# A fused attention and two-layer feed-forward kernel: one w_in unit, w_out's units and block 0's y change their places

## The chip, the cores and the metric

One core of one Trainium2 chip. The metric is the device time of one execution in microseconds (us). Engines: TensorE (PE, with its weight loads PEld), VectorE (DVE), ScalarE (ACT), GpSimd (POOL), and SyncE (SP), whose queue issues the DMAs here.

## What is computed

Four batches of 8-head attention (half of the heads with a local mask, half with a strided one), a first feed-forward part without a nonlinearity between its products, and a second one with a sigmoid gelu:

```python
# attention: q, k, v of 4 x 8 x 576 x 64, masks per head
x = softmax(scale * q @ k.T, masked) @ v       # 2304 tokens x 512
a = x @ w1                                     # 512 x 1024
b = x @ w2
y = (a * b @ w3) @ w_out                       # 1024 x 1024, 1024 x 512
h = y @ w_in                                   # 512 x 2048
out = (h / (1 + exp(-1.702 * h))) @ w_out2     # 2048 x 512
```

All in float32.

## The kernel before

Products run on TensorE at reduced operand width, so that every float32 factor is split into a high part (ScalarE, L246, `split_hi`) and a low part (VectorE, L252, `split_lo`), and each product is three matmuls (high x low, low x high, high x high). The weights arrive as raw 64-bit words and are turned into float32 on ScalarE and VectorE. The large last product, with w_in and w_out of the second part, is done by a fast matrix scheme with seven products of quarters, for which sums of the weights' quarters are made first.

The weights of that last part are converted in eight units each, in stages in which TensorE is doing something else:

- w_in units (`u_placed`, L1098): two conversions on ScalarE (L1111, L1112), three steps on VectorE (L1113 to L1115), the sums (L1106, L1093, L1108), a write-back to DRAM (L1117), and the load of the unit two further on (L1088). Their places are in `UNITS_Y` (batch 1's y) and `UNITS_2` (batch 2).
- w_out units (`wo_steps`, L1120): two conversions (ScalarE, L1144, L1145), three steps on VectorE (L1146 to L1148), three sums (L1133, L1093), two high splits (`high`, ScalarE), two low splits (`low`, VectorE), two stores (L1128). Unit 0 is made at the end of batch 2's stage from `EARLY_AT` on, units 1 to 6 in batch 3's stage, unit 7 in the last one.

The stages around the change, by the time in the profile: batch 1's y (201 to 260), batch 2's products with the last attention pairs (260 to 334), the end of batch 2's y and batch 3 (334 to 429), the last products (429 on). Within a stage every engine's order is written by hand: each piece of work has a place in units of one TensorE step of 12 matmuls, the pieces are sorted by place, and each engine (TensorE, VectorE, ScalarE, SyncE) runs its own in that order and waits only for what it needs:

```python
for _, _, f in sorted((at, n, f) for n, (at, f) in enumerate(steps)):
    f()
```

A product pair (`pieces`, L1224) of batch 2 or 3 for chunk m of 8 and half hb has its places from `at = 24 * hb + 2 * m`: first product (`one(0)`, at), its copy by ScalarE out of the accumulator (L1234, at + 0.99), second product (at + 1), multiply by VectorE (L1237, at + 1.99), high split (at + 2.4), low split (at + 2.75). The eight pairs of a half feed its y products (L1173; in batch 3 `fourth`, L1354): in the first half at steps 16 to 24, in batch 2's second half they are moved to the start of batch 3's list (`over`, places less 48, from -8), behind everything of batch 2's. The accumulators (`mm`) rotate over four.

An attention pair (`placed`, L673) at place u has the products of the pair before and its own scores on TensorE (`trip`), the mask and maximum on VectorE (L546), exponentials on ScalarE (L556), the normalisation (L565 to L567), 32x32 transposes on VectorE for a local head (L583) or on TensorE for a strided one (L589). Pair 10 has two local ones; pair 11 is only the last product.

Block 0's y for the last part is read back in two halves kk and split in `y_steps` (L1312), placed at `at + gaps`. `early_y` (L1283) opens the space for it and issues the loads of w_out unit 1 and of y; `early_load` issues that of unit 0; `wo_load` those of units 2 to 6, each into a space that an earlier piece has to leave first.

Of the kernel before, what the change touches and what calls it, by code (L numbers as in the profile page):

```python
# [51 lines left out]
BODY = 0x7FFFFFF8  # L52
REBIAS = 2.0 ** -112
LOW = 2.0 ** -29
PAIRS_Y = ((4, 2.6), (5, 12.8), (6, 25.6))
UNITS_Y = ((0, 8.3), (1, 17.0), (2, 21.2), (3, 30.3))
PAIRS_2 = ((7, 2.4), (8, 10.6), (9, 19.8), (10, 28.4), (11, 37.0))
UNITS_2 = ((4, 6.4), (5, 15.6), (6, 24.2), (7, 31.8))
PAIR_AT = (0.05, 0.12, 0.2, 0.32, 0.42, 0.55, 0.72)
EARLY = 8  # L60
EARLY_AT = 35.6
AHEAD = 6
PACED = 50
MOVED = {
# [148 lines left out]
def body(ctx: ExitStack, tc, qk, vv, mask, ql, vl, qs, vs, qmask, w1, w2, w3t, wo, win, wout, out):  # L213
# [27 lines left out]
    def r(ap):  # L241
        return ap.bitcast(F32)
# [75 lines left out]
    def room(what, n, w, tag, bufs):  # L318
        if what + str(n) in lent:
            return lent[what + str(n)]  # L320
        return aq.tile([P, w], F32, tag=tag, name=tag, bufs=bufs)
# [769 lines left out]
    def both_minus(out, a, x):  # L1091

        nc.vector.tensor_tensor(  # L1093
            out.rearrange("p (n c) -> p n c", n=2), a.unsqueeze(1).to_broadcast([P, 2, 256]),
            x[:, :7 * 256].rearrange("p (n c) -> p n c", c=256)[:, 0:5:4], op=ALU.subtract,
        )
# [20 lines left out]
            (u + 3, sums), (u + 4.2, lambda: nc.sync.dma_start(widram[i], x[:, 256:])),  # L1117
        ]

    def wo_steps(u, raw, room, high_room=None, late=0):  # L1120
        view = lambda t: raw().bitcast(t).rearrange("p (n t) -> p n t", t=2)
        hi = lambda: (high_room or raw)().bitcast(F32R)[:, :7 * 256]
        xi = lambda: room()[:, :CW2].bitcast(I32)
        part = lambda n: room()[:, n * 256:(n + 1) * 256]
        B12, B11, B21, B22, S1, S3, S2 = range(7)

        def store(s, t):
            nc.sync.dma_start(  # L1128
                tdram[:, u // 2, :, u % 2, s].rearrange("j p n -> p j n"), t.rearrange("p (j n) -> p j n", j=7)
            )  # L1130

        def sum_(o, a, b, op):
            nc.vector.tensor_tensor(part(o), part(a), part(b), op=op)  # L1133

        def low(n):
            c = slice(n * 896, (n + 1) * 896)
            split_lo(room()[:, c].bitcast(F32R), room()[:, c], hi()[:, c])

        def high(n):
            c = slice(n * 896, (n + 1) * 896)  # L1140
            split_hi(hi()[:, c], room()[:, c])

        return [
            (-0.6, lambda: nc.scalar.activation(view(I32)[:, :, 0], view(U32)[:, :, 0], AF.Copy, scale=LOW)),  # L1144
            (0.1, lambda: nc.scalar.activation(room()[:, :CW2], view(F32)[:, :, 1], AF.Copy, scale=REBIAS)),  # L1145
            (0.8, lambda: nc.vector.tensor_scalar(xi(), xi(), 3, BODY, op0=ALU.logical_shift_left, op1=ALU.bitwise_and)),  # L1146
            (1.25, lambda: nc.vector.scalar_tensor_tensor(xi(), view(I32)[:, :, 1], SIGN, xi(), op0=ALU.bitwise_and, op1=ALU.bitwise_or)),
            (2.05, lambda: nc.vector.tensor_tensor(xi(), xi(), view(I32)[:, :, 0], op=ALU.add)),  # L1148
            (2.65 + late / 2, lambda: sum_(S1, B12, B22, ALU.add)),
            (2.75 + late / 2, lambda: both_minus(room()[:, 5 * 256:7 * 256], part(B11), room())),  # L1150
            (3.1 + late / 2, lambda: sum_(B12, B21, S2, ALU.add)),
            (3.45 + late, lambda: high(0)),
            (3.9 + late, lambda: high(1)),
            (4.05 + late, lambda: low(0)),
            (4.35 + late, lambda: store(0, r(hi()))),
            (4.8 + late, lambda: low(1)),
            (5.4 + late, lambda: store(1, room()[:, :7 * 256])),
        ]

    cvs = ExitStack()  # L1160
# [137 lines left out]
            early[1] = cv[0].tile([P, 2 * CW2], F32, tag="x", name="x", bufs=2)  # L1298
        return early[1]

    steps2 += [(27.0, early_load), (38.6, early_y)]
    steps2 += [(EARLY_AT + g, f) for g, f in wo_steps(0, lambda: early[0], early_room, None, 1.6)]
    written(steps2)
    cvs.close()
    xbs_stack.close()
# [74 lines left out]
    )  # L1380
    sums = early["sums"]
    steps3.append((-6.9, lambda: ys.update({0: y_load(0, 0, rooms[1])})))
    for kk, at in ((1, -0.9), (0, 2.2)):
        gaps = (0.05, 1.0, 1.4, 0.1, 0.75, 0.8, 1.85, 2.0, 2.85)
        steps3 += [(at + g, f) for g, f in zip(gaps, y_steps(kk, ys))]

    def wo_load(u):
        todo3[u] = rooms[(0, 1, 2, 0, 1, 0)[u - 2]]()
        nc.sync.dma_start(todo3[u], wout[u])

    UNIT = 8.0
    for u in range(1, NU):
        at = -5.8 if u == 1 else 6 + UNIT * (u - 2)
        if 1 < u < NU - 1:
            steps3.append((((2.6, 5.5, 5.7)[u - 2] if u < 5 else at - 14), lambda u=u: wo_load(u)))
        if u < NU - 1:
            steps3 += [(at + g, f) for g, f in wo_steps(u, lambda u=u: todo3[u], lambda u=u: sums[:, u % 2])]
    for n, (lo, hi, a, b, c) in enumerate(((4, 6, 32.1, 40.2, 41.6), (5, 7, 40.05, 46.9, 47.7))):
        lo, hi = slot[lo][:, :7 * 256], slot[hi][:, :7 * 256]
        steps3 += [  # L1400
# [57 lines left out]
    class Split:  # L1458
# [4 lines left out]
        def hi(self):  # L1463
            self.t = self.room or p2.tile([P, 2, HT], F32R, tag="sp", name="sp", bufs=7)
            split_hi(self.t[:, 0], self.src())
# [304 lines left out]
```

## Time and profile before

| what | us |
|---|---|
| median of 3 runs | 791.58 |
| the runs | 789.95, 791.58, 793.72 |
| the profiled execution | 791.2 |
| its span, first to last instruction | 789.4 |
| TensorE busy | 770.6 (98%) |
| VectorE busy | 580.8 (74%) |
| ScalarE busy | 480.2 (61%) |
| mean granted TensorE clock | 0.996 of 2.4 GHz |

The span is that of one execution, with some 1.8 us around it. A row of an instruction list has its start and duration; what stands in brackets is how long the engine had been idle and what ended that. A row of the table of waits says who waited for whom. In the busy tables a stretch is given with the busy us of each engine, the granted share of TensorE's clock (1.00 is 2.4 GHz, 0.50 is 1.2 GHz) and the DMA engines' share.

### The profile page before, as it was taken

The page shows a single profiled execution, that of the slowest core. Times are in us where ns is not written, and L with a number is a line of the kernel's source. Part 1 is how long each engine was busy: PE and PEld are TensorE (multiplying, and loading weights), DVE is VectorE, ACT ScalarE, POOL GpSimd, SP SyncE. Part 2 cuts the span into 40 slices and gives each one's busy share as a digit, 9 for nine tenths or more (in the row PEclk, how much of TensorE's full clock was granted, in tenths as well). Part 3 has the DMA queues.
Part 4 walks back from the last instruction along what each step waited for, and adds up shares of the span by engine and source line. Part 5 has one row for each costly group of instructions (what it writes and reads, how often), then busy time and mean ns, then how long its engine had stood idle before and what let it go on. Part 6 is the DMA issues. An engine that isn't in the chain of part 4 may idle for free.

```text
span 789.4 us, 16754 instructions
## 1 busy us (share of the span) xinstructions
PE 770.6 (98%) x6545; PEld 747.6 (95%) x6545; DVE 580.8 (74%) x1248; ACT 480.2 (61%) x1041; POOL 5.8 (1%) x14
## 2 busy tenths in 40 slices
PE   5899999999999999989999999999999999999998
PEld 4899999987999999988999999999999999999998
DVE  4899678788778686977776788794677794577743
ACT  5877646477565554554465767673666674666552
POOL 2000000000000000000000000000000000000000
PEclk9999999999999999999999999999999999999999
DMA  8887455632788546296998837789254489343382
GB/s 281 293 307 237 163 172 176 206 125 83 255 270 285 176 144 218 83 296 203 243 274 235 329 134 249 285 280 383 105 203 150 155 282 374 113 160 112 113 280 89
DMA packets 72078, 168.14 MB, mean 213 GB/s; under 512 B 6336, under 2 KB 45248, under 8 KB 69440
## 3 DMA queue, kind: packets, MB, share of 16 engines
q1 hardware_dynamic: 71856, 167.04, 63.2%
q8 instruction: 51, 0.84, 0.4%
q14 instruction: 27, 0.22, 0.1%
q10 hardware_dynamic: 144, 0.04, 0.0%
HBM read 130.88 MB, written 36.18 MB: 212 GB/s over the span
## 4 chain that ended last, share of the span: by engine, by line
PE 84%; DMA 5%; DVE 4%; ACT 4%; issue 1%; SPq 1%; ACTq 0%; DVEq 0%
PE acc L1508 23%; PE ps L1497 22%; PE ps L716 20%; PE ps L1173 8%; PE acc L1354 3%; PE acc L1019 3%; PE sc L533 1%; DMA sums<-ydram 1%; PE pv L602 1%; DMA tdram<-raw 1%; DMA raw<-in_wout 1%; ACT w L246 1%; DVE w L252 1%; DVE xw L809 1%; ACT xw L801 1%
## 5 line engine op out<-in xcount | busy, mean ns | idle before, releaser
L1508 PE MATMUL acc<-w,sp 128*128 128x256 f32 x1440 | 179.5, 282 | 0.0
L1508 PEld LDWEIGHTS acc<-w,sp 128*128 128x128 f32 x1440 | 177.8, 191 | 0.0
L1497 PE MATMUL ps<-yq,hl 128*128 128x384 f32 x924 | 168.1, 335 | 0.0
L1497 PEld LDWEIGHTS ps<-yq,hl 128*128 128x128 f32 x924 | 158.7, 188 | 0.9 <-DVE part L1453 0.6
L252 DVE TENSOR_TENSOR sp<-part,sp 128x384 fp32r<-128x384 f32 x136 | 71.5, 554 | 59.1 <-ACT sp L246 59.1
L716 PE MATMUL ps<-xbh,w 128*128 128x288 f32 x512 | 102.6, 295 | 0.0
L716 PE MATMUL ps<-xah,w 128*128 128x288 f32 x512 | 102.2, 294 | 0.0
L716 PEld LDWEIGHTS ps<-xbh,w 128*128 128x128 f32 x512 | 81.9, 188 | 1.3 <-issue 0.7
L1173 PE MATMUL ps<-ab,w 128*128 128x288 f32 x576 | 80.7, 300 | 2.2 <-DVE ab L252 2.1
L716 PEld LDWEIGHTS ps<-xah,w 128*128 128x128 f32 x512 | 82.0, 188 | 0.0
L1173 PEld LDWEIGHTS ps<-ab,w 128*128 128x128 f32 x576 | 78.2, 191 | 3.3 <-DVE ab L252 2.4
L716 PE MATMUL ps<-xal,w 128*128 128x288 f32 x256 | 76.5, 299 | 1.3 <-ACT abf L1234 0.7
L716 PE MATMUL ps<-xbl,w 128*128 128x288 f32 x256 | 76.9, 300 | 0.6 <-issue 0.6
L1450 ACT ACTIVATE part<-part 128x384 f32<-128x384 f32 x72 | 37.9, 526 | 61.4 <-DVE part L1453 61.3
L246 ACT ACTIVATE sp<-part 128x384 fp32r<-128x384 f32 x136 | 64.1, 517 | 11.3 <-PE acc L1508 10.3
L246 ACT ACTIVATE ab<-abf 128x288 fp32r<-128x288 f32 x64 | 27.3, 439 | 39.5 <-DVE abf L1237 37.1
L716 PEld LDWEIGHTS ps<-xal,w 128*128 128x128 f32 x256 | 48.0, 188 | 2.6 <-ACT abf L1234 1.1
L716 PEld LDWEIGHTS ps<-xbl,w 128*128 128x128 f32 x256 | 48.0, 188 | 0.9
L1019 PE MATMUL acc<-w,w 128*128 128x512 f32 x192 | 45.6, 396 | 0.2
L1019 PEld LDWEIGHTS acc<-w,w 128*128 128x128 f32 x192 | 35.8, 188 | 9.2 <-ACT raw L1025 1.0
L252 DVE TENSOR_TENSOR hl<-fetched,hl 128x1024 fp32r<-128x1024 f32 (+1 forms) x40 | 43.3, 1083 | 0.0
L246 ACT ACTIVATE w<-xw 128x512 fp32r<-128x512 f32 (+1 forms) x30 | 23.3, 775 | 29.2 <-DVE xw L809 28.3
(193 smaller groups left out, 1117.3 us busy)
## 6 DMA issues: line engine op xcount, KB each, us to landing
w<-tdram SPq DMA_DIRECT2D x84, 512.0 KB, 4.6
fetched<-widram SPq DMA_DIRECT2D x20, 896.0 KB, 6.2
raw<-in_win SPq DMA_DIRECT2D x8, 1024.0 KB, 5.5
widram<-x SPq DMA_DIRECT2D x8, 896.0 KB, 5.5
raw<-in_wout SPq DMA_DIRECT2D x7, 1024.0 KB, 5.2
tdram<-raw SPq DMA_DIRECT2D x6, 896.0 KB, 5.5
tdram<-sums SPq DMA_DIRECT2D x6, 896.0 KB
raw<-in_w3t SPq DMA_DIRECT2D x10, 512.0 KB, 4.5
```

What stands on the lines that cost most here:

```text
L246: nc.scalar.activation(hi, src, AF.Copy)
L252: e.tensor_tensor(lo, src, r(hi), op=ALU.subtract)
L533: nc.tensor.matmul(sc[:nq, g, i * P:i * P + nk], qs[rows, i], ks[rows, i], start=True, stop=True,)
L602: nc.tensor.matmul(pv[rows, h // 2, :nq], L["v"][:nk, h * D:(h + 1) * D], ps[:nk, h * nq:(h + 1) * nq], start=True, stop=True,)
L716: nc.tensor.matmul(ps, ws[a][m // 2][:, at:at + P], xh[c][:, k, cols], start=(k == 0 and (a, c) == ORDER[0]), stop=(k == KC - 1 and (a, c) ...
L801: "a": lambda xf, rf, ri, ru, x, hi, lo: nc.scalar.activation(xf, rf[:, :, 1], AF.Copy, scale=REBIAS),
L1019: nc.tensor.matmul(acc[f], hl[:, a, f * P:(f + 1) * P], wor[c][g], start=(g == 0 and (a, c) == ORDER[0]), stop=(g == MC - 1 and (a, c) == ...
L1173: nc.tensor.matmul(yacc[n], wfs[a][k][:, n * P:(n + 1) * P], hold[s % 2, k][:, c], start=(k == 0 and (a, c) == ORDER[0]), stop=(k == MC - ...
L1354: nc.tensor.matmul(st[0], wfs[a][k][:, n * P:(n + 1) * P], hold[hb, k][:, c], start=(k == 0 and (a, c) == ORDER[0]), stop=(k == MC - 1 and ...
L1450: nc.scalar.activation(out(), src(), func)
L1497: nc.tensor.matmul(ps, w[a][:, f * 256 + kk * P:f * 256 + (kk + 1) * P], yq[:, b, kk, c], start=(first and kk == 0 and (a, c) == ORDER[0]) ...
L1508: nc.tensor.matmul(to, g.t[:, a, t * P:(t + 1) * P], t3[:, i % 2, c], start=(opens and i == 0 and n == 0 and t % 2 == 0), stop=(i == NU - ...
```

## The change

Batch 1's y gets a fifth w_in unit (unit 4, from batch 2's list), its units and pairs are placed anew; batch 2 keeps units 5 to 7, and its pairs 9 to 11 come 0.8 to 1.4 steps sooner. `early_load` goes from 27.0 to 24.5, `early_y` from 38.6 to 37.4. w_out unit 0 begins at 34.9 instead of 35.6, and its sums, splits and stores are no longer set off by `late` (0.8 and 1.6 steps). In batch 3's list block 0's y halves go from -0.9 and 2.2 to -0.7 and 3.2, with smaller gaps; w_out's units 2 to 6 go from 6 + 8 (u - 2) to 8 + 7.75 (u - 2), the loads of units 3 and 4 go one step later, and from unit 2 on the second high split, the stores and the second low split stand half a step further behind.

```diff
--- before.py
+++ after.py
@@ -52,13 +52,13 @@
 BODY = 0x7FFFFFF8
 REBIAS = 2.0 ** -112
 LOW = 2.0 ** -29
-PAIRS_Y = ((4, 2.6), (5, 12.8), (6, 25.6))
-UNITS_Y = ((0, 8.3), (1, 17.0), (2, 21.2), (3, 30.3))
-PAIRS_2 = ((7, 2.4), (8, 10.6), (9, 19.8), (10, 28.4), (11, 37.0))
-UNITS_2 = ((4, 6.4), (5, 15.6), (6, 24.2), (7, 31.8))
+PAIRS_Y = ((4, 2.6), (5, 12.6), (6, 27.2))
+UNITS_Y = ((0, 8.0), (1, 16.6), (2, 20.2), (3, 24.0), (4, 31.4))
+PAIRS_2 = ((7, 2.4), (8, 10.6), (9, 19.0), (10, 27.2), (11, 35.6))
+UNITS_2 = ((5, 6.4), (6, 15.4), (7, 23.0))
 PAIR_AT = (0.05, 0.12, 0.2, 0.32, 0.42, 0.55, 0.72)
 EARLY = 8
-EARLY_AT = 35.6
+EARLY_AT = 34.9
 AHEAD = 6
 PACED = 50
 MOVED = {
@@ -1117,7 +1117,7 @@
             (u + 3, sums), (u + 4.2, lambda: nc.sync.dma_start(widram[i], x[:, 256:])),
         ]
 
-    def wo_steps(u, raw, room, high_room=None, late=0):
+    def wo_steps(u, raw, room, high_room=None, apart=0):
         view = lambda t: raw().bitcast(t).rearrange("p (n t) -> p n t", t=2)
         hi = lambda: (high_room or raw)().bitcast(F32R)[:, :7 * 256]
         xi = lambda: room()[:, :CW2].bitcast(I32)
@@ -1146,15 +1146,15 @@
             (0.8, lambda: nc.vector.tensor_scalar(xi(), xi(), 3, BODY, op0=ALU.logical_shift_left, op1=ALU.bitwise_and)),
             (1.25, lambda: nc.vector.scalar_tensor_tensor(xi(), view(I32)[:, :, 1], SIGN, xi(), op0=ALU.bitwise_and, op1=ALU.bitwise_or)),
             (2.05, lambda: nc.vector.tensor_tensor(xi(), xi(), view(I32)[:, :, 0], op=ALU.add)),
-            (2.65 + late / 2, lambda: sum_(S1, B12, B22, ALU.add)),
-            (2.75 + late / 2, lambda: both_minus(room()[:, 5 * 256:7 * 256], part(B11), room())),
-            (3.1 + late / 2, lambda: sum_(B12, B21, S2, ALU.add)),
-            (3.45 + late, lambda: high(0)),
-            (3.9 + late, lambda: high(1)),
-            (4.05 + late, lambda: low(0)),
-            (4.35 + late, lambda: store(0, r(hi()))),
-            (4.8 + late, lambda: low(1)),
-            (5.4 + late, lambda: store(1, room()[:, :7 * 256])),
+            (2.65, lambda: sum_(S1, B12, B22, ALU.add)),
+            (2.75, lambda: both_minus(room()[:, 5 * 256:7 * 256], part(B11), room())),
+            (3.1, lambda: sum_(B12, B21, S2, ALU.add)),
+            (3.45, lambda: high(0)),
+            (3.9 + apart, lambda: high(1)),
+            (4.05, lambda: low(0)),
+            (4.35 + apart, lambda: store(0, r(hi()))),
+            (4.8 + apart, lambda: low(1)),
+            (5.4 + apart, lambda: store(1, room()[:, :7 * 256])),
         ]
 
     cvs = ExitStack()
@@ -1298,8 +1298,8 @@
             early[1] = cv[0].tile([P, 2 * CW2], F32, tag="x", name="x", bufs=2)
         return early[1]
 
-    steps2 += [(27.0, early_load), (38.6, early_y)]
-    steps2 += [(EARLY_AT + g, f) for g, f in wo_steps(0, lambda: early[0], early_room, None, 1.6)]
+    steps2 += [(24.5, early_load), (37.4, early_y)]
+    steps2 += [(EARLY_AT + g, f) for g, f in wo_steps(0, lambda: early[0], early_room)]
     written(steps2)
     cvs.close()
     xbs_stack.close()
@@ -1380,21 +1380,21 @@
     )
     sums = early["sums"]
     steps3.append((-6.9, lambda: ys.update({0: y_load(0, 0, rooms[1])})))
-    for kk, at in ((1, -0.9), (0, 2.2)):
-        gaps = (0.05, 1.0, 1.4, 0.1, 0.75, 0.8, 1.85, 2.0, 2.85)
+    for kk, at in ((1, -0.7), (0, 3.2)):
+        gaps = (0.05, 0.8, 1.2, 0.1, 0.75, 0.8, 1.85, 1.9, 2.6)
         steps3 += [(at + g, f) for g, f in zip(gaps, y_steps(kk, ys))]
 
     def wo_load(u):
         todo3[u] = rooms[(0, 1, 2, 0, 1, 0)[u - 2]]()
         nc.sync.dma_start(todo3[u], wout[u])
 
-    UNIT = 8.0
+    UNIT = 7.75
     for u in range(1, NU):
-        at = -5.8 if u == 1 else 6 + UNIT * (u - 2)
+        at = -5.8 if u == 1 else 8 + UNIT * (u - 2)
         if 1 < u < NU - 1:
-            steps3.append((((2.6, 5.5, 5.7)[u - 2] if u < 5 else at - 14), lambda u=u: wo_load(u)))
+            steps3.append((((2.6, 6.5, 6.7)[u - 2] if u < 5 else at - 14), lambda u=u: wo_load(u)))
         if u < NU - 1:
-            steps3 += [(at + g, f) for g, f in wo_steps(u, lambda u=u: todo3[u], lambda u=u: sums[:, u % 2])]
+            steps3 += [(at + g, f) for g, f in wo_steps(u, lambda u=u: todo3[u], lambda u=u: sums[:, u % 2], None, 0.5 if u > 1 else 0)]
     for n, (lo, hi, a, b, c) in enumerate(((4, 6, 32.1, 40.2, 41.6), (5, 7, 40.05, 46.9, 47.7))):
         lo, hi = slot[lo][:, :7 * 256], slot[hi][:, :7 * 256]
         steps3 += [
```

## Rows read from the trace of the kernel before

**Rows 1.** Who waited for whom, TensorE: us in total, times, longest us.

```profile
PE ps L1173 <- DVE ab L252: 2.1, 1, 2.1
```

**Rows 2.** Busy table by stage: busy us (instructions) per engine, clock, DMA.

```profile
201.00:260.00 59.00, 58.96 (x495) 57.23 (x493) 46.05 (x142) 37.49 (x109) 0.00 (x0) 1.00 0.82 273
260.00:334.00 74.00, 74.00 (x638) 72.02 (x637) 59.16 (x185) 39.75 (x122) 0.00 (x0) 1.00 0.45 153
351.00:429.00 78.00, 76.75 (x574) 75.86 (x573) 58.07 (x86) 43.01 (x69) 0.00 (x0) 1.00 0.84 243
```

**Rows 3.** The same table in 2 us windows, behind the gap at 337.

```profile
340.00:342.00 2.00, 2.00 (x10) 2.00 (x9) 1.52 (x2) 2.00 (x4) 0.00 (x0) 0.50 0.45 146
342.00:344.00 2.00, 2.00 (x13) 2.00 (x12) 1.31 (x2) 0.63 (x1) 0.00 (x0) 0.69 1.11 271
```

**Rows 4.** TensorE's instructions in order: start, us, line, tile, [idle <-releaser].

```profile
329.97 0.88 PE L602 MATMUL pv<-band,v 128*64 128x96 f32 x16
334.04 2.92 PE L1173 MATMUL ps<-ab,w 128*128 128x288 f32 x21
339.09 6.18 PE L1173 MATMUL ps<-ab,w 128*128 128x288 f32 x33 [2.12 <-DVE ab L252]
...
366.99 0.40 PE L716 MATMUL ps<-xal,w 128*128 128x288 f32 x1 [0.36 <-ACT abf L1234]
...
369.41 0.40 PE L716 MATMUL ps<-xal,w 128*128 128x288 f32 x1 [0.58 <-DVE abf L1237]
...
374.95 0.40 PE L716 MATMUL ps<-xal,w 128*128 128x288 f32 x1 [0.30 <-ACT abf L1234]
```

**Rows 5.** VectorE's instructions, end of batch 2's stage.

```profile
315.67 0.29 DVE L546 CUSTOM_DVE_ANT_0 sm<-sc,msk 96x128 f32<-96x128 f32 x1 [2.96 <-PE sc L533]
...
323.13 0.45 DVE L1237 TENSOR_TENSOR abf<-ps,abf 128x288 f32<-128x288 f32 x1
323.50 1.87 DVE L583 STREAM_TRANSPOSE band<-sm 32x128 f32<-32x128 f32 x6
...
325.78 0.69 DVE L1113 TENSOR_SCALAR x<-x 128x1024 int32<-128x1024 int32 x1
...
331.03 0.45 DVE L1237 TENSOR_TENSOR abf<-ps,abf 128x288 f32<-128x288 f32 x1
331.40 0.68 DVE L1146 TENSOR_SCALAR x<-x 128x1024 int32<-128x1024 int32 x1
...
337.62 0.45 DVE L1237 TENSOR_TENSOR abf<-ps,abf 128x288 f32<-128x288 f32 x1
338.58 0.46 DVE L252 TENSOR_TENSOR ab<-abf,ab 128x288 fp32r<-128x288 f32 x1 [0.51 <-ACT ab L246]
339.42 2.10 DVE L252 TENSOR_TENSOR x<-x,raw 128x896 fp32r<-128x896 f32 x2 [0.38 <-ACT raw L246]
```

**Rows 6.** ScalarE's instructions, the same stretch and batch 3's first half.

```profile
328.12 0.45 ACT L246 ACTIVATE ab<-abf 128x288 fp32r<-128x288 f32 x1 [2.74 <-DVE abf L1237]
328.47 0.39 ACT L1234 ACTIVATE abf<-ps 128x288 f32<-128x288 f32 x1
328.76 1.16 ACT L1144 ACTIVATE raw<-raw 128x1024 int32<-128x1024 uint32 x1
329.81 1.17 ACT L1145 ACTIVATE x<-raw 128x1024 f32<-128x1024 f32 x1
...
338.45 1.78 ACT L246 ACTIVATE raw<-x 128x896 fp32r<-128x896 f32 x2
...
364.15 1.14 ACT L1144 ACTIVATE raw<-raw 128x1024 int32<-128x1024 uint32 x1 [2.33 <-DMA raw<-in_wout]
...
366.52 0.41 ACT L1234 ACTIVATE abf<-ps 128x288 f32<-128x288 f32 x1
```

**Rows 7.** The busy table in 2 us windows, in the opening.

```profile
20.00:22.00 2.00, 0.67 (x15) 0.54 (x14) 1.90 (x6) 0.91 (x2) 0.00 (x0) 1.00 0.95 326
22.00:24.00 2.00, 1.66 (x18) 1.54 (x18) 1.84 (x5) 1.92 (x6) 0.00 (x0) 0.60 0.84 284
```

## The prediction

> **What bounds the kernel now.** I read the waits of TensorE first, then the busy table by stage, then the instruction lists around each wait. TensorE waits for another engine for long only once after the opening: 2.1 us, for VectorE's `ab` [rows 1]. The table by stage shows it busy for 58.96 of 59 us in the stage of batch 1's y and for all 74 us of batch 2's products; in batch 3's stage it misses 1.25 of 78 us [rows 2]. So VectorE is worth something only where TensorE meets an empty input: at the seam of batches 2 and 3, and in batch 3's first half.
>
> The seam: batch 2's last y products start at 334.04, and TensorE stands from 336.97 to 339.09 [rows 4]. It wants the low split of the last product pair (m = 7), which VectorE ends at 339.04 [rows 5]. The product itself was there at 334.04; its multiply ran at 337.62, because w_out unit 0 stood ahead of it in VectorE's order. Then the clock falls from 2.4 to 1.2 GHz: the granted share is 0.50 from 340 to 342 and 0.69 from 342 to 344 [rows 3]. At half rate 2 x 0.50 + 2 x 0.31 = 1.62 us of work is lost there. The seam costs 2.12 + 1.62 = 3.74 us.
>
> Batch 3: three gaps of 0.36, 0.58 and 0.30 us [rows 4], together 1.24. ScalarE stood 2.33 us at w_out unit 2's first conversion, which waited for its load until 364.15, and the copy that frees TensorE's accumulator came behind it at 366.52 [rows 6]. All that the change can win is 3.74 + 1.24 = 4.98 us, 0.63% of the profiled execution's 791.2 us.
>
> **The change part by part.**
>
> *A w_in unit moves to batch 1's y.* In VectorE's list unit 7 begins at 325.78 and the next multiply at 331.03 [rows 5]; with two 0.37 us visitors taken out it costs 5.25 - 0.74 = 4.5 us. VectorE goes from 46.05 to some 50.6 busy of 59 us in the y stage and from 59.16 to 54.7 of 74 in batch 2's [rows 2]. The splits of y's input are placed four to five product steps ahead of their products; a step is 1.60 us (pair 11's product from 329.97, 0.88, and two steps fill the time to 334.04 [rows 4]); TensorE is full there now. The moved unit's load, its write-back and the two refills it triggers go with it on SP's queue, and the last y input loads (step 20) are ahead of the new unit (24.0). I cost it at 0; if a unit did push a split past its four steps (6.4 us), the bound is the whole unit, 4.5 us.
>
> *Unit 0 of w_out begins sooner.* Pair 10's attention goes from step 28.4 to 27.2, one product step: 315.67 - 1.60 = 314.07. From there to the multiply of m = 3 took 323.13 - 315.67 = 7.46 us; now its second transposes (1.87) stand ahead of that multiply, as does the multiply of m = 1 (0.37): 314.07 + 9.70 = 323.77 [rows 5]. From there ScalarE sets the pace: split of m = 3 at 324.25 (0.48 later, the multiply's 0.45 and a hand-over), copy at 324.60 (0.35, from 328.12 to 328.47), unit 0's first conversion at 324.89 (0.29), split of m = 4 at 325.94 (1.05), copy 326.29, second conversion 326.58, ready at 327.75 (1.17) [rows 6]. So VectorE begins unit 0 at 327.78 instead of 331.40 [rows 5]: 3.62 us sooner.
>
> *But its low splits now stand ahead of the last multiply.* With `late` gone they are placed at 38.95 and 39.70; before, at 41.25 and 42.0, behind it (39.99). From unit 0's first VectorE instruction to the end of the last low split took 339.04 - 331.40 = 7.64 us. Three things are added: the multiply of m = 5 (0.37, it stood just ahead at 331.03), the two splits (2.10, the row at 339.42) [rows 5], and a wait. ScalarE runs unit 0's first high split (38.35) ahead of the split of m = 6 (38.40), so VectorE, which wants m = 6 next, stands from the end of unit 0's sums: hand-over 0.10, high split 0.89 (half of 1.78 [rows 6]), split of m = 6 and hand-over 0.48, together 1.4. Queued behind that wait are unit 0's low splits and then the last multiply, for which TensorE waits. 327.78 + 7.64 + 0.37 + 2.10 + 1.4 = 339.3.
>
> So the head start of 3.62 is spent on 3.87 of work and waiting, and the last low split ends at 339.3 against 339.04. The unknown is how much of the 1.4 runs beside other waits. Bounds: none hidden, 339.3; all hidden, 337.9. A floor from TensorE agrees: the second conversion stands behind the copy of m = 5, whose product ends where step 35 begins, 334.04 less five steps and pair 11's 0.88, 325.16, which gives 325.16 + 0.3 + 0.3 + 1.17 = 326.9 and an end at 338.4 with the 1.4, 337.0 without. I take 339.3, +0.3 us, because nothing in the order lets ScalarE pass. The clock then falls as before: a gap as long at the same place.
>
> *The load of unit 1 and of y* are issued some steps sooner; unit 1's first conversion stands behind the split of m = 7 on ScalarE either way, and now without the 1.78 us of high splits between [rows 6]. Its stores and so the load of unit 2 come about a microsecond sooner. 0 by itself.
>
> *Block 0's y 1.0 step and unit 2 two steps further behind.* Unit 2's first conversion is placed at 7.4 instead of 5.4, behind the copy (6.99) that came at 366.52. That copy then follows the multiply of m = 2, and stands near 364.0, 2.6 us ahead of when TensorE wants the accumulator (366.99 - 0.36 = 366.63). The next multiply (7.99) is ahead of unit 2 on VectorE too. All three gaps go: -1.24. What is late next: unit 2 (from step 8) against the copy of m = 4, wanted three steps later; units 3 to 6 come at most 1.75 steps later with 7.75 between, the last ends near step 45 of 48, and its factors are held back until the next stage's sixth quad. If the unit blocks there again: 0 of the 1.24. `apart` lets the copy of the next m go between two high splits: 0.
>
> Sum on the profiled execution: 791.2 + 0.3 - 1.24 = 790.3. The median of the runs shown, 791.58, lies 0.4 above that execution, so 790.6 for the median.
>
> **The rivals.** *The gap shrinks and the clock stays.* If the 1.4 us wait hides and ScalarE has the conversions at its floor, the end is 337.0 to 338.4, a gap of 0 to 1.4. The opening has a gap of 1.33 us in the window 20 to 22, followed by a grant of 0.60 [rows 7], so it would have to be short. At a gap of 0.7: -1.42 - 1.62 - 1.24 = -4.3, 787.3 for the median; at none 786.6. For it: VectorE is 4.5 us emptier in this stage. Against: the order on ScalarE and the two splits in front.
>
> *The gap stays, the clock does not fall.* Then -0.94 - 1.62 = -2.6, 789.0. The trace shows one fall behind each of two long gaps [rows 3, 7], so I give it little. The Trainium skill, "TensorE: Matmul & The Clock Gate", Part 1, says that the gate's timing runs free of the kernel, so that one kernel can differ from run to run; by that rule the 1.62 us could fall away with the same gap. No run of before here shows a gap of 2 us without a fall.
>
> *Slower: the splits in front without the head start.* If ScalarE's conversion of unit 0 is held as it was (second conversion at 329.81 [rows 6]), unit 0 begins at 331.4 and the added 3.87 lie wholly on TensorE's gap: 2.12 becomes 6.0 us. With the 1.24 won: +2.6, and a second stretch at half rate as long as the first +1.6: 791.2 + 4.2, 795.8 for the median. It decides at unit 0's first VectorE instruction: break-even is 0.94 behind the forecast's place, 328.7; later than that is slower than before. The chain of ScalarE steps above speaks against; that the chain starts with a multiply VectorE reaches late speaks for.
>
> *The change does not do what it says in batch 3:* the gaps return at other units: 791.9.
>
> **How the numbers follow.** Forecast 0.57 (790.6, own range 789.3 to 791.8 with the runs' scatter); shrunk gap 0.17 (787.3); clock spared 0.11 (789.0); splits in front 0.09 (795.8); no gain in batch 3 0.06 (791.9). A measurement of this kernel tells about 0.5%, 4.0 us, from no change. Faster by more than that holds most of the second case, 0.14; slower most of the fourth, 0.08; the rest is 0.78. The range reaches from the middle of the shrunk gap, 786.8, to part of the slower case, 794.0.
>
> **What would show it.** In the changed profile: unit 0's first VectorE instruction near 327.8, its two 896-wide low splits ahead of the last multiply, TensorE's gap at 337 between 1.5 and 2.6 us with half clock behind it; ScalarE's copy of m = 3 ahead of unit 2's conversion and no gap between 366 and 376; VectorE some 50 of 59 us busy in the y stage with no gap of TensorE. The forecast is wrong if the gap at 337 is under 1 us or over 3.5, or if the y stage shows TensorE waiting.

## The result and the profile after

The changed kernel took 797.1 us in the median (795.78 to 798.37) against 791.7 for the kernel before beside it: a ratio of 1.0069, 95% interval 1.0057 to 1.0081. It is slower, where 790.6 with a range from 786.8 to 794.0 had been forecast. Its profiled execution has a span of 795.3 us, 5.9 more than before.

First the table of waits of TensorE after the opening (who waited for whom: us in total, times, longest):

```profile
PE ps L1497 <- ACT z L1562: 4.8, 1, 4.8
...
PE ps L1173 <- DVE ab L252: 2.2, 1, 2.2
...
PE pt L589 <- DVE sm L567: 0.8, 1, 0.8
...
PE ps L716 <- ACT abf L1234: 0.3, 1, 0.3
```

The second line is the seam's wait of [rows 1], still there. The first and the third are new: a stop of 4.8 us in the last stage, which no step of the prediction looks at, and one of 0.8 in the stage of batch 1's y. The same four in TensorE's list (start, us, line, tile, idle before and releaser), against [rows 4]:

```profile
261.89 0.62 PE L589 MATMUL pt<-ident,sm 126*126 126x126 f32 x4 [0.83 <-DVE sm L567]
...
341.50 3.70 PE L1173 MATMUL ps<-ab,w 128*128 128x288 f32 x26 [2.20 <-DVE ab L252]
...
412.30 0.40 PE L716 MATMUL ps<-xal,w 128*128 128x288 f32 x1 [0.33 <-ACT abf L1234]
...
428.30 5.82 PE L1497 MATMUL ps<-yq,w 128*128 128x384 f32 x30
438.94 8.15 PE L1497 MATMUL ps<-yq,w 128*128 128x384 f32 x36 [4.82 <-ACT z L1562]
```

The busy table of after by stage, as in [rows 2], and in 2 us windows, first behind the seam's gap, as in [rows 3], then around the new stop (busy us of PE, PEld, DVE, ACT, POOL, granted share of the clock, DMA share, GB/s):

```profile
201.00:260.00 59.00, 58.97 (x490) 56.98 (x489) 47.97 (x142) 38.23 (x111) 0.00 (x0) 1.00 0.86 292
260.00:334.00 74.00, 73.17 (x631) 71.00 (x630) 59.69 (x188) 40.09 (x123) 0.00 (x0) 1.00 0.45 159
```

```profile
340.00:342.00 2.00, 0.50 (x4) 0.50 (x4) 0.93 (x3) 1.46 (x2) 0.00 (x0) 1.00 1.09 263
342.00:344.00 2.00, 2.00 (x18) 2.00 (x17) 0.34 (x1) 1.43 (x2) 0.00 (x0) 1.00 1.16 299
...
436.00:438.00 2.00, 0.00 (x0) 0.00 (x0) 0.00 (x0) 0.00 (x0) 0.00 (x0) 0.50 0.98 308
438.00:440.00 2.00, 1.06 (x3) 1.07 (x4) 0.67 (x2) 0.90 (x2) 0.00 (x0) 0.50 1.04 368
440.00:442.00 2.00, 2.00 (x8) 2.00 (x8) 0.91 (x2) 0.67 (x2) 0.00 (x0) 0.50 0.96 386
442.00:444.00 2.00, 2.00 (x12) 2.00 (x11) 1.52 (x2) 1.39 (x3) 0.00 (x0) 0.87 1.03 428
```

Behind the seam's gap the clock stayed at 2.4 GHz this time; from within the stop in the last stage it was at 1.2 GHz until about 442.5.

Where the 5.9 us of the two profiled executions come from, by the starts of TensorE's stages:

| up to | before | after | later by | of it |
|---|---|---|---|---|
| the y stage's first product (L1173) | 201.20 | 202.57 | 1.37 | scatter of the opening, see below |
| the seam's restart (L1173) | 339.09 | 341.50 | 1.04 | y stage's gap 0.83, seam's gap 0.08; 0.13 not placed |
| the last stage's first product (L1497) | 429.20 | 428.30 | -3.31 | no half clock at the seam -1.62, batch 3's gaps 1.24 to 0.33, -0.91; 0.78 not placed |
| its first product with w_in's factor `hl` | 446.2 | 452.2 | 6.9 | the stop 4.82, half clock behind it 1.8; 0.3 not placed |
| the end of the span | 789.4 | 795.3 | -0.1 | |

The first line is outside the change: the code up to there is the same, and another kernel of this study with the whole change in it (the y tiles elsewhere, below) reached that product at 201.42.

Why the last stage stops: SP's queue in the kernel before, then in the kernel after, then ScalarE after (L1128 are the stores of a w_out unit, here unit 6; L1363 the four stores of y; L1436 loads of factors):

```profile
422.69 0.36 SPq L1128 DMA_DIRECT2D tdram<-raw  x1
424.74 0.36 SPq L1128 DMA_DIRECT2D tdram<-sums  x1
425.19 4.96 SPq L1363 DMA_DIRECT2D ydram<-ysb  x4
430.25 1.94 SPq L1436 DMA_DIRECT2D w<-tdram  x2
```

```profile
427.12 0.36 SPq L1128 DMA_DIRECT2D tdram<-raw  x1
428.40 0.36 SPq L1128 DMA_DIRECT2D tdram<-sums  x1
428.86 5.17 SPq L1363 DMA_DIRECT2D ydram<-ysb  x4
434.12 0.89 SPq L1436 DMA_DIRECT2D w<-tdram  x2
...
438.39 0.49 ACT L1562 ACTIVATE z<-ps 128x384 f32<-128x384 f32 x1 [5.65 <-DMA ydram<-ysb]
```

Unit 6's two stores are issued 4.43 and 3.66 us later than before. The last four stores of y, written behind them, wait, although the first tile's copy was done at 427.4: 428.86 instead of 425.19 for the first. ScalarE's copy z of the last stage's first quad stood 5.65 us for a landing of these stores. What has z to do with y? By the semaphores in the trace, the instruction ahead of z waits for the first of the four stores, and that one's last part came in at 438.29, 0.1 us ahead of z. Its tile lies in a pool (`p1`, L1360) that is closed at the end of the stage, and the pool of z (`p2`, L1412) is opened behind it. This is the first theory (A): **unit 6's lateness holds SP's queue, the stores of y stand behind it, and a tile of the next stage waits for the memory that they still read.**

The same semaphores tell the parts of this wait: of the 10.9 us from the end of that tile's copy to the landing, SP's queue held the store for 1.5, and for 9.4 it was under way, to land 0.2 us behind unit 6's second store (438.08).

The rivals: that unit 6's bytes crowd the DMA engines, whatever the order (C); and that unit 6's lateness costs by itself, whoever waits for it (D).

### The profile page after: what moved, and what is told of

Same layout as the page of the kernel before. It is cut to its first block, busy times and chain, and to the rows that moved or that the text cites. A ratio compares the mean times of both kernels' runs of the same rounds, so it can differ in the third digit from the quotient of the medians.

```text
span 795.3 us, 16746 instructions
## 1 busy us (share of the span) xinstructions
PE 770.9 (97%) x6545; PEld 747.6 (94%) x6545; DVE 581.1 (73%) x1248; ACT 479.2 (60%) x1041; POOL 5.8 (1%) x14
## 4 chain that ended last, share of the span: by engine, by line
PE 69%; DVE 13%; DMA 7%; ACT 6%; issue 3%; SPq 0%; ACTq 0%; DVEq 0%
PE acc L1508 23%; PE ps L1497 22%; PE ps L716 12%; PE ps L1173 6%; PE acc L1019 3%; DVE w L252 1%; DMA rawx<-in_w 1%; DMA raw<-in_w 1%; DVE xw L809 1%; DMA ydram<-ysb 1%; ACT w L246 1%; PE sc L533 1%; DVE band L583 1%; DMA abdram<-abf 1%; PE pv L602 1%
## 5 line engine op out<-in xcount | busy, mean ns | idle before, releaser
L1497 PE MATMUL ps<-yq,hl 128*128 128x384 f32 x924 | 168.1, 335 | 0.0
L1497 PEld LDWEIGHTS ps<-yq,hl 128*128 128x128 f32 x924 | 158.6, 188 | 0.9 <-DVE part L1453 0.3
L1173 PE MATMUL ps<-ab,w 128*128 128x288 f32 x576 | 79.1, 296 | 2.2 <-DVE ab L252 2.2
L1173 PEld LDWEIGHTS ps<-ab,w 128*128 128x128 f32 x576 | 76.7, 188 | 3.4 <-DVE ab L252 2.4
```

What stands on the lines that cost most here:

```text
L1173: nc.tensor.matmul(yacc[n], wfs[a][k][:, n * P:(n + 1) * P], hold[s % 2, k][:, c], start=(k == 0 and (a, c) == ORDER[0]), stop=(k == MC - ...
L1497: nc.tensor.matmul(ps, w[a][:, f * 256 + kk * P:f * 256 + (kk + 1) * P], yq[:, b, kk, c], start=(first and kk == 0 and (a, c) == ORDER[0]) ...
```

## The experiments

The kernel before beside them had a median of 791.98, 792.58, 792.06 and 792.27 us in the four groups of runs. "Undone" means the lines of before at that place.

**Batch 3's part alone, and all but it.** The first has the kernel before with the last hunk of the diff (block 0's y, w_out's places and loads) and `apart`; the second the kernel after without these.

> The kernel before with batch 3's part of the change alone (block 0's y, w_out units 2 to 6 and their loads, the half step between splits). Theory A: the gap at the start of the last stage comes with this part, 4 to 5 us and 2 us at half clock, less the 0.9 us of gaps won in batch 3's first half: 796.5 to 797.5. Theory B: no new gap at the last stage, 790.5.

> The changed kernel with batch 3's part undone: only the w_in unit, the attention pairs, unit 0 and the early loads are moved. Theory A: no gap at the last stage; the gap of 2.2 us at the seam and the one of 0.8 us at the end of batch 1's y stay, batch 3's gaps of about 1 us come back: 791 to 793. Theory B: the gap of 4.8 us stays, 798.

Alone: 797.36 us, 1.0066 (1.0048 to 1.0084), with a stop of 4.75 us at the same place, and the seam as before. Undone: 793.38, 1.0013 (0.9997 to 1.0029), no stop in the last stage, batch 3's gaps 0.59 and 0.29 back, the y stage's gap 1.03. So the loss comes with batch 3's part and hardly with the rest.

**Unit 6 at its old place.** After, with

```diff
-        at = -5.8 if u == 1 else 8 + UNIT * (u - 2)
+        at = -5.8 if u == 1 else 38 if u == 6 else 8 + UNIT * (u - 2)
```

and unit 6's `apart` at 0 (its load, placed at `at - 14`, moves with it).

> The changed kernel with w_out unit 6 alone put back to step 38 without the half step between its splits; everything else stays as changed. Theory A (the two stores of unit 6 hold the four y stores behind them on SP's queue, and the last stage's first quad copies into memory that the last of these y tiles still holds): the gap of 4.82 us at the start of the last stage and the half clock behind it (2.1 us) go, some 790.2 us, 6.9 less than the changed kernel. Theory B (the gap comes from elsewhere, the fifth w_in unit's load or the moved block 0 y): the gap stays, 797.

Measured 794.8 us, 1.003 (1.0011 to 1.0049), with a stop of 2.35 us. Half of it went. Unit 5, left where it was, still came late on VectorE, and unit 6 behind it: its second store was issued 1.97 us ahead of the last stage's first product, where before it was 4.46 ahead. Direction right, size not.

**The last two y tiles in other memory.** After, with

```diff
-            ysb = (p1, cv_b)[n // 2].tile([P, HB], F32, tag="ysb", name="ysb", bufs=2)
+            ysb = p1.tile([P, HB], F32, tag="abf", name="ysb", bufs=3) if hb and n > 1 else (p1, cv_b)[n // 2].tile(
+                [P, HB], F32, tag="ysb", name="ysb", bufs=2)
```

> The changed kernel, but the last two y tiles of batch 3 lie in p1, in memory that the last stage's first quad does not take over; unit 6 is as late and SP's queue as full as in the changed kernel. Theory A (memory still held by a store that was issued late): the gap of 4.82 us shrinks to under 1.5 us (unit 6's own raw tile lies in the same pool, and its store was issued at 427.1), 790 to 792 us. Theory C (unit 6's late splits crowd ScalarE and VectorE where the last stage begins): the gap stays at 4 to 5 us, 797.

Measured 801.91 us, 1.0122 (1.008 to 1.0163). TensorE and ScalarE:

```profile
439.46 11.82 PE L1497 MATMUL ps<-yq,w 128*128 128x384 f32 x54 [9.12 <-ACT s L1562]
...
438.92 0.49 ACT L1562 ACTIVATE s<-ps 128x384 f32<-128x384 f32 x1 [9.68 <-DMA ydram<-ysb]
```

The stop did not go; it moved. The two tiles moved are the third and the fourth, and z waits for the first, which stayed. The pool `p1` is closed there too, and with the fourth tile in it the wait stands at the copy s, two copies earlier than z: the instruction ahead of s waits for the last store, which landed at 438.82. That the wait follows the tile's memory speaks for A's last link; the number expected was wrong, since the wrong tiles were moved, and into memory that is taken over as well. Memory that stays free of the last stage was not tried: the space for two tiles that outlive it isn't there.

**Unit 6's stores behind the stores of y.** After, with both stores of unit 6 at place 48.1:

```diff
-            (4.35 + apart, lambda: store(0, r(hi()))),
+            (held or 4.35 + apart, lambda: store(0, r(hi()))),
...
-            (5.4 + apart, lambda: store(1, room()[:, :7 * 256])),
+            (held or 5.4 + apart, lambda: store(1, room()[:, :7 * 256])),
```

> The kernel after, with one thing changed: unit 6's two stores are written behind the last four stores of y on SP's queue (place 48.1 instead of 41.35 and 42.4 or so). Unit 6's arithmetic, the copies of y and the memory that they lie in stay. Theory A (unit 6's stores hold SP's queue, the four small stores of y come behind them, and the memory of the last two y tiles, which the last stage's first quad takes over, comes free late): the four are issued from 427.1 on at about 1.3 us each, done before ScalarE asks for the memory, so the gap of 4.82 us ahead of the last stage's first z product falls under 0.5 and the half clock behind it (some 2.05 us lost) goes: 797.1 - 4.82 - 2.05 = about 790.2 us (789 to 791.5). Theory D (the loss is unit 6's lateness in itself, whoever waits): its stores now come later still, at about 432.5 and 433.8, and the factors read back from them are late at the last stage's sixth quad: the gap moves there, 795 to 799.

Measured 796.23 us, 1.005 (1.0037 to 1.0063): not 790.2. SP's queue and TensorE:

```profile
428.06 2.98 SPq L1363 DMA_DIRECT2D ydram<-ysb  x4
431.10 0.44 SPq L1128 DMA_DIRECT2D tdram<-raw  x1
431.63 0.60 SPq L1128 DMA_DIRECT2D tdram<-sums  x1
432.32 2.62 SPq L1436 DMA_DIRECT2D w<-tdram  x2
...
443.14 1.42 PE L1508 MATMUL acc<-w,sp 128*128 128x256 f32 x9 [1.90 <-DMA w<-tdram]
```

The stop at z is gone (ScalarE's z waits 0.34 us, for its own u): ahead of unit 6's stores the first store of y lands 2.47 us after its issue, at 430.53, where it took 9.43 in after. So what stood ahead of it in the queue made the stop, A's middle link. But the order takes away two things at once, the 1.5 us that SP held the store and unit 6's bytes ahead of it; by these times most of the wait was the bytes, and C has its share. And the factors that the queue loads next, w, now come behind 1.8 MB of stores, their landing 10.6 us after the issue instead of 4.8 before, and TensorE stands for them 1.90 us, then 1.19 for a copy. Theory D has a share: **whatever is last in the queue pays.** It takes an earlier unit 6, not another order.

**The stores of y from ScalarE.** After, with `(nc.scalar if hb else nc.sync).dma_start(...)` for the last four.

> The kernel after, with the last four stores of y issued by ScalarE behind its own copies instead of by SP; unit 6's stores stay where they are on SP's queue. Theory A: the stores of y no longer stand behind unit 6's; the last copy ends at 429.9, so they are issued by about 430.5 instead of 432.89. Their packets still share the DMA engines with unit 6's 1.8 MB, so the landing is taken as 4.5 to 7 us behind the issue, 434.5 to 437: the gap of 4.82 falls to between 0.5 and 3, with the half clock gone or halved: 791 to 795 us, 792.5 as the middle. Theory C (it is the crowding of the DMA engines by unit 6's bytes, not the order on the queue): the landing stays at 438, 796 to 798.

Measured 797.27 us, 1.0056 (1.0042 to 1.0071), a miss. The stop is 3.14 us, but earlier, at the copy s: an issue holds ScalarE itself, up to 1.18 us, and the last two copies of y run at 431.71 and 432.56 instead of from 429.17 on, with the last stage's behind them. It is the total that C forecast, but not for C's reason: the first store of y, issued at 428.01 by ScalarE, ahead of unit 6's second one (429.00), landed at 433.89 and not at 438, and nothing waited for it. The last two, issued behind it, took 9.5 and 9.4 us to land.

```profile
428.88 1.18 ACTq L1363 DMA_DIRECT2D ydram<-ysb  x1
...
434.31 12.49 PE L1497 MATMUL ps<-yq,w 128*128 128x384 f32 x54 [3.14 <-ACT s L1562]
```

The Trainium skill says in "DMA: Bandwidth & Descriptors", section "Issuing engines are not separate DMA queues", that transfers from several issuing engines share the same DMA engines and that only the issuing time is saved; this run agrees, with 797.27 us for 797.1 and the 9.5 and 9.4 us above, and shows that time to be worth a place on a busy engine.

**Units 3 to 6 sooner.** After, with

```diff
-        at = -5.8 if u == 1 else 8 + UNIT * (u - 2)
+        at = (-5.8, 8, 15, 22.5, 30, 38)[u - 1] if u < NU - 1 else 46
```

and `apart` for units 2 to 4 only (the loads of units 5 and 6, placed at `at - 14`, move with them).

> The kernel after, with units 3 to 6 of batch 3 at places 15, 22.5, 30 and 38 instead of 15.75, 23.5, 31.25 and 39, and units 5 and 6 with their last steps close together again; unit 2, block 0's y and the loads stay at the places of after. Theory A (unit 6's lateness is unit 5's and 4's lateness handed on, and every 1 us by which its second store comes behind 4.5 us ahead of the last stage's first product costs 1 us there): unit 6's stores are issued at about 422.7 and 424.8 again, the four stores of y behind them in time, the last stage has no gap over 0.5 and no half clock: 797.1 - 4.82 - 2.05 = about 790.2 us, with the y stage's gap and the seam's still there. Theory D (the loss moves to whoever waits for unit 6's bytes, as it moved to the factors' loads where the stores of y went first): any unit 6 that starts behind place 38 shows it; here too nothing should be left: D and A part only if a gap on w<-tdram stays. Rival: unit 2 at 8 and unit 3 at 15 crowd VectorE and batch 3 shows gaps of 1 us or more again: 791 to 793.

Measured 794.06 us, 1.0013 (0.9996 to 1.003), a stop of 1.73 us: again less late, again not enough. Place 38 is not what it was: TensorE, with its gaps in batch 3 closed, and no longer held by them, is nearer behind. Nine of the kernels have the stores of unit 6 ahead of the stores of y on SP's queue and the y tiles where they were. Their traces give how far ahead of the last stage's first product the second store was issued, how far behind that product the first store of y had landed (from its semaphore), and the stop:

| kernel | second store issued | first product L1497 | ahead by | y landed behind by | stop at z |
|---|---|---|---|---|---|
| both repairs, units sooner, W0 behind (below) | 419.31 | 424.85 | 5.54 | 2.44 | none |
| batch 3 undone, both repairs (below) | 423.40 | 427.88 | 4.48 | 2.93 | none |
| before | 424.74 | 429.20 | 4.46 | 2.99 | none |
| batch 3 undone | 428.17 | 432.40 | 4.23 | 3.26 | none |
| units 3 to 6 sooner | 428.26 | 431.12 | 2.86 | 6.46 | 1.73 |
| the same with both repairs (below) | 422.39 | 424.41 | 2.02 | 6.87 | 2.13 |
| unit 6 at its old place | 427.52 | 429.49 | 1.97 | 7.07 | 2.35 |
| after | 428.40 | 428.30 | -0.10 | 9.99 | 4.82 |
| batch 3's part alone | 427.15 | 426.97 | -0.18 | 10.02 | 4.75 |

The stop follows the landing: it is "y landed behind by" less 4.7 us in three rows, and less 5.2 and 5.3 in the last two. The lead of the second store tells it roughly only: from 2.86 ahead to 0.18 behind, 3.04 us, the stop grows by 3.02, but between 2.86 and 2.02 by 0.40, and a lead of 4.23 has no stop. For the first store of y lands 0.2 to 0.4 us behind unit 6's second one in all nine, 7.4 to 9.9 us after the latter's issue. By the landing, the kernel before had an estimated 1.7 to 2.3 us to spare (4.7 to 5.3 less its 2.99).

**The two other gaps.** On top of the kernel with unit 6's stores behind: first unit 0's sums moved by 1.15 and its splits and stores by 2.3 steps, behind the last multiply, its first steps staying early; then pair 6 at 25.6 with the y stage's unit 3 at 26.1, behind it:

```diff
-    steps2 += [(EARLY_AT + g, f) for g, f in wo_steps(0, lambda: early[0], early_room)]
+    steps2 += [(EARLY_AT + g, f) for g, f in wo_steps(0, lambda: early[0], early_room, None, 0, None, 2.3)]
...
-PAIRS_Y = ((4, 2.6), (5, 12.6), (6, 27.2))
+PAIRS_Y = ((4, 2.6), (5, 12.6), (6, 25.6))
-UNITS_Y = ((0, 8.0), (1, 16.6), (2, 20.2), (3, 24.0), (4, 31.4))
+UNITS_Y = ((0, 8.0), (1, 16.6), (2, 20.2), (3, 26.1), (4, 31.4))
```

> The kernel with unit 6's stores behind the stores of y, and on top of it unit 0's sums and splits back behind the other work of the seam (the spacing that the kernel before had, its first steps staying as early as in the kernel after). If the seam's gap of 2.20 us is ScalarE and VectorE doing unit 0's splits ahead of the sums that TensorE wants, it closes: 790.2 - 2.2 = about 788.0 us. Rival: the splits only move the wait into units 1 and 2, whose first steps follow: the gap closes and batch 3 shows 1 to 2 us of new waits: 789 to 790.5.

> The same, and pair 6 of the y stage at place 25.6 (as in the kernel before) instead of 27.2, with unit 3 behind it at 26.1 instead of 24.0. If the y stage's gap of 0.83 us is unit 3's VectorE steps, delayed by the wait for a buffer that unit 1's write-back holds, standing ahead of pair 6's masks, it closes: 788.0 - 0.83 = about 787.2 us. Rival: unit 3, now later, delays unit 4 and a new gap opens in the y stage's last third: 788 to 789.

Measured 794.21 (1.0017, 1.0004 to 1.003), then 792.29 (1.0003, 0.9993 to 1.0014). The seam's gap is gone in the first, 2.0 us for a gap of 2.19; the new waits in batch 3 are two of 0.22. The y stage's gap is gone in the second, 1.9 us for a gap of 0.96; in its profile the wait for w (2.03) has the clock at 1.00 behind it, where the other's (2.11) has 0.73 and 0.50 in the two windows from 442 to 446, so that part of the 1.9 is the clock's; a new wait of 0.82 us, for `hl`, took some back. The step each expected is right, and the levels are 5 to 6 us above those expected, by the last stage, as in the kernel that they build on.

**Both repairs without that.** With units 3 to 6 sooner, and with batch 3's part undone:

> The same with the two other repairs: unit 0's sums and splits behind the other work of the seam, and pair 6 at 25.6 with unit 3 of the y stage behind it at 26.1. From the two gaps that these took away where they were tried (2.1 to 2.2 us at the seam, 0.9 in the y stage): 790.2 - 2.2 - 0.9 = about 787 us (786 to 789), some 0.6% under the kernel before. Rival: the seam's later splits push units 1 to 6 back again and the last stage shows part of its gap: 789 to 791.

> The kernel with the batch-3 part undone (793.4 us), with the same two repairs. What is left of the change is then the moved unit of w_in and unit 0's earlier first steps. 793.4 - 2.2 (seam) - 1.0 (y stage) - up to 1.6 (the half clock behind the seam's gap) = 788.6 to 790.2; batch 3 keeps gaps of about 0.9. If the kernel with units 3 to 6 back is faster than this one by about 0.9 us, the batch-3 part is worth just its gaps.

The first: 790.7 us, 0.999 (0.9975 to 1.0006), and it came out as the rival had it: the last stage stops for 2.13 us. The second: 789.01, 0.9958 (0.9944 to 0.9971), without a stop, and faster than before. With the same two repairs the kernel that keeps batch 3's part is the slower one: closing 0.8 us of gaps in batch 3 (1.17 to 0.35) opens 2.1 in the last stage.

**Batch 3's part with room for unit 6.** The first of these two, with units 5 and 6 at 29.4 and 36.8 and the low split of the last stage's first w_in unit (W0, 2.02 us of VectorE) behind unit 6's sums and splits:

```diff
-        at = (-5.8, 8, 15, 22.5, 30, 38)[u - 1] if u < NU - 1 else 46
+        at = (-5.8, 8, 15, 22.5, 29.4, 36.8)[u - 1] if u < NU - 1 else 46
...
-    for n, (lo, hi, a, b, c) in enumerate(((4, 6, 32.1, 40.2, 41.6), (5, 7, 40.05, 46.9, 47.7))):
+    for n, (lo, hi, a, b, c) in enumerate(((4, 6, 32.1, 40.2, 42.15), (5, 7, 40.05, 46.9, 47.7))):
```

> The kernel with units 3 to 6 back and both repairs (790.7 us, where the last stage's gap was still 2.13 us and its half clock about 1 us), with units 5 and 6 earlier still (29.4 and 36.8) and the low split of w_in's first unit of the last stage (2.02 us of VectorE) behind unit 6's sums instead of ahead of them (42.15 instead of 41.6). Theory A: unit 6's second store, which there was issued 2.0 us ahead of the last stage's first product, is issued over 4 us ahead of it, the stores of y follow in time, the gap goes with its half clock: 790.7 - 2.1 - 1.0 = about 787.6 us; then the place of the one unit is shown to be all that batch 3's part has against it. Rival: the raw copies of unit 6 (0.9 us each on ScalarE) now stand between batch 3's own copies and TensorE waits there, 0.5 to 1.5 us: 788 to 789.5, no better than the kernel with batch 3's part undone (789.0).

Measured 787.66 us, 0.9946 (0.9928 to 0.9963). SP's queue and TensorE's last stage:

```profile
417.66 0.36 SPq L1128 DMA_DIRECT2D tdram<-raw  x1
419.31 0.36 SPq L1128 DMA_DIRECT2D tdram<-sums  x1
420.72 5.08 SPq L1363 DMA_DIRECT2D ydram<-ysb  x4
...
424.85 11.94 PE L1497 MATMUL ps<-yq,w 128*128 128x384 f32 x66
```

No stop from 424.85 on, and the clock at 1.00 in the windows there. A wait of 0.68 at 405.65 for a copy is the rival's, smaller than what was won. This kernel and the one with batch 3 undone both beat the kernel before; their intervals overlap, so which of the two is the better is not told.

## Why the prediction was wrong, point by point

- **Unit 0 and the two splits in front: right.** Unit 0's first VectorE step is at 330.12, and the last multiply at 340.02 behind the two splits. In VectorE's list of after:

```profile
330.12 0.70 DVE L1146 TENSOR_SCALAR x<-x 128x1024 int32<-128x1024 int32 x1 [0.90 <-ACT x L1145]
...
337.64 0.46 DVE L252 TENSOR_TENSOR ab<-abf,ab 128x288 fp32r<-128x288 f32 x1 [1.41 <-ACT ab L246]
338.02 2.09 DVE L252 TENSOR_TENSOR x<-x,raw 128x896 fp32r<-128x896 f32 x2
340.02 0.45 DVE L1237 TENSOR_TENSOR abf<-ps,abf 128x288 f32<-128x288 f32 x1
```

  The wait for the split of m = 6 is 1.41 us (1.4 was worked out), the splits 2.09. TensorE's gap is 2.20 for 2.12. Against TensorE, whose last y products start 2.33 us later here (336.37 for 334.04), unit 0 began 3.61 us sooner (3.62 was worked out). [rows 4, 5] were read rightly; the runs with the splits behind show that just these closed it.
- **The clock behind that gap: a rival had it.** No half clock followed in this execution, 1.62 us that the forecast had put down as lost. It falls behind such a gap in some executions and not in others (last section), so the 0.11 for it was too little. It was set against two falls, one of them behind "a gap of 1.33 us" in the opening; in the trace those are two gaps, 0.48 us up to 20.52 and 1.19 up to 22.34.
- **Batch 3: right.** The copy of m = 3 is ahead of unit 2's conversion, and the three gaps are gone; one of 0.33, at 412.30, is new:

```profile
365.98 0.39 ACT L1234 ACTIVATE abf<-ps 128x288 f32<-128x288 f32 x1
366.27 1.14 ACT L1144 ACTIVATE raw<-raw 128x1024 int32<-128x1024 uint32 x1
```

- **The w_in unit moved at cost 0: wrong by 0.83 us.** The bound looked at the splits of y's input; what came late was an attention pair. ScalarE, VectorE and SP in the y stage of after:

```profile
242.22 0.42 SPq L1117 DMA_DIRECT2D widram<-x  x1
...
248.79 1.12 ACT L1111 ACTIVATE x<-raw 128x1024 f32<-128x1024 f32 x1 [2.08 <-DMA widram<-x]
...
249.95 0.69 DVE L1113 TENSOR_SCALAR x<-x 128x1024 int32<-128x1024 int32 x1 [2.12 <-ACT x L1111]
...
254.99 0.42 DVE L1108 TENSOR_TENSOR x<-x 128x256 f32<-128x256 f32 x1
```

  Unit 3, at 24.0 instead of 30.3, wants one of two buffers that unit 1's write-back, issued at 242.22, gives back at 248.8. Its VectorE steps, 249.95 to 255.4, then stand ahead of pair 6's masks and normalisation (L567 at 261.06), for which TensorE waits at 261.89. The prediction counted the write-back's place on SP's queue and not the buffer that it holds. VectorE has 47.97 us in this stage where 50.6 was expected: unit 4's steps begin at 261.66, so they fall behind 260 and show in the next row, 59.69 where 54.7 was expected. TensorE waiting in this stage is one of the signs that the prediction itself had set for being wrong.
- **"The last ends near step 45 of 48, and its factors are held back until the next stage's sixth quad": this is the step that failed.** It costed units 3 to 6 at 0 by who reads their factors. Their stores were not followed on SP's queue, where four small stores stand behind them and land behind them, nor these to the memory that they read and the next stage takes over. Nor was the time checked: the kernel before had an estimated 1.7 to 2.3 us to spare there. Against it, unit 6's second store came 3.66 us later (its place is one step, 1.6 us, later, and the splits are set apart), TensorE came 0.90 us sooner, and from that store's issue to the landing of y's first it took 9.89 us instead of 7.45: 7.00 together, of which 4.82 are the stop, with 1.8 of half clock behind it. Why the landing took 2.44 us longer is not shown. With batch 3's part undone, and its 0.9 us of gain with it, the change stands at 793.38.
- **The range.** The slower rival was put at the seam, with a condition that did not come about; no case was held open in the last stage, since no row of it was read.

What stays open: 0.78 us of the gain between the seam and the last stage; why unit 6 at place 38 again begins 11.3 us ahead of the last stage's first product instead of 13.8 (413.09 and 424.41 with units sooner and both repairs; 415.44 and 429.20 before), of which the closed gaps explain about 0.8; and which of the last run's two moves brings how much.

## What to carry to other kernels

When a step is moved, follow each of its transfers twice: along the queue that issues it, to what is queued behind it, and to the memory that those read or free, into the next stage. "Its result is needed only later" says nothing on this; the slack is the time between the landing of what stands behind that transfer in the queue and the moment its memory or data are wanted, and it can be read off the trace before the move (here about 2 us, against 7.0 that the change took). A gap closed ahead of a fixed chain takes its time out of that slack.

## What the runs showed of the hardware

- **The clock behind a gap of one length.** Behind the seam's gap of 2.12 to 2.20 us the granted share fell, to between 0.50 and 0.57 in the lowest 2 us window, in before and five of the kernels here, and not in after (2.20), with unit 6 at its old place (2.20) and with y's stores from ScalarE (2.19). After and the kernel with unit 6's stores behind have the same order up to there, and a gap of 2.20 and 2.19; the second shows (2 us windows, as above):

```profile
342.00:344.00 2.00, 2.00 (x10) 2.00 (x10) 0.07 (x1) 1.46 (x3) 0.00 (x0) 0.50 1.16 301
344.00:346.00 2.00, 2.00 (x13) 2.00 (x12) 1.93 (x3) 0.00 (x0) 0.00 (x0) 0.68 1.05 143
```

  The Trainium skill, "TensorE: Matmul & The Clock Gate", Part 1, has the gate's timing independent of the kernel, so that one kernel differs from run to run; these two agree.
- **Issuing is not free behind large stores.** Four stores of 144 KB took SP 5.17 us behind unit 6's two of 896 KB each, and 2.98 ahead of them, where the queue was nearly empty. The copies' arrival enters these too; a single issue took 1.14 to 1.38 us behind them and 0.32 to 1.12 ahead of them.
- **A small store behind large ones lands with them.** The first of these 144 KB stores landed 2.47 us after its issue ahead of unit 6's two, and 9.43 us after it behind them; in the nine kernels of the table it landed 0.18 to 0.42 us behind unit 6's second store.
